# Spectral products by adding transfers, and a new order of the butterflies, in two FFT-convolution layers

## The chip, the cores and the metric

The kernel runs on one core of a Trainium2 chip. The metric is the time of one execution on the device in microseconds; runs of one kernel agree within about 0.1%, and the median of three is taken. The profile is of one execution.

## The reference

Four layers follow one another, each adding its result to `x`, which has L = 2048 rows and D = 640 columns:

- layers a and c: normalize each row, then convolve each of the 640 columns causally with its own kernel of length 2048 (a sum of 128 damped exponentials), and add a multiple of the input;
- layers b and d: normalize each row, then multi-query attention of 32 heads of width 20 (one key and value for all).

```python
Kf = rfft2(Kp[:, None, :])                # the kernel, padded to 2L
Uf = rfft2(up[:, :, None, :])             # the normalized input, padded to 2L
y = irfft2(Uf * Kf[None], s=(1, 2 * L))[:, :, 0, :L]
x = x + (y.transpose(0, 2, 1) + u * Dskip)
```

The change is in layers a and c alone. Their kernel spectra are worked out once, in layer a, and kept in DRAM.

## The kernel before

**Tiling.** The 640 columns are cut into five chunks of 128 (`NCH = 5`, `c` = 0 to 4). A chunk's spectrum is one tile `A` of 128 partitions x 16 x 256 numbers (2 MB). The 16 slots are eight sub-transforms with a real and an imaginary slot each.

**A chunk's steps**, each on its own engine:

- ScalarE scales the rows of x into a tile `xn` of which there is one buffer (`normals`, L736; 24 instructions of 128x128);
- PE multiplies `xn` by the weights `wf` (`dense`, L565; 64 matmuls, which the trace counts as 128 instructions), and ScalarE copies the four results out of PSUM into `A` (L581). Chunk 0 and the kernel's own spectra use `raw` (L538) instead, whose first butterflies (`radix`, L555) run on VectorE;
- VectorE (DVE in the profile) does the forward butterflies, `fft8(..., -1)` at L90: 16 instructions between `A`, a second tile `B` and a half-size tile `R`. Its first two read all of slots 0 to 7; its seventh is the first that writes `R`;
- VectorE multiplies by the kernel's spectrum `kh` (`product`, L750): two products into `B` and `R` and a subtraction, two products and an addition, and then the first two inverse butterflies, eight instructions of 128x2048 at L751;
- VectorE does the other inverse butterflies, `fft8(..., +1)`: 16 instructions;
- PE does the inverse matmuls with the weights `wi` (`inverse`, L764) in four groups of 16 matmuls, whose results go alternately to two PSUM banks;
- VectorE adds each group to `x` (`residual`, L782). For chunk 3 the group starts with a matmul that brings `x` in (L769), and ScalarE copies it back (L785).

**Order.** On PE, ScalarE and VectorE the instructions run in the order in which the program writes them; the other queues (SP and POOL) take theirs as they come ready. Each engine's queue is in order. `weave` (L133) puts a list of calls between the instructions of another list, at given places. `turn(g)` (L829) does the residual of group g and, for g = 0 and 1, writes PE's group g + 2. The loop at L807 does for each chunk: product and inverse butterflies (with turns 2 and 3 of the chunk before woven in), groups 0 and 1 of the inverse, forward butterflies of the next chunk (turns 0 and 1 woven in), scaling and `dense` of the chunk after next. So `dense` stands on PE behind all four inverse groups of the chunk.

**Buffers.** Two spectra `A`, two kernel spectra `kh` (loaded two chunks ahead by SP, L680), one `B`, one `R`.

**Around it.** While chunk 3 and 4 are done, ScalarE works out sums and squares of `x` for the next layer's normalization (`stats_first`, L609), and in layer a the attention weights are split into two parts on PE and ScalarE (`attn_weights`, L871; "the weight splitting"), woven into chunk 4's product. In layer a the kernel's own spectra come first (`kernel_spectra`, L685): raw transforms, butterflies and a store of each to DRAM.

Of the kernel before, what the change touches and what calls it, by code (L numbers as in the profile page):

```python
# [11 lines left out]
F32 = mybir.dt.float32  # L12
# [4 lines left out]
ALU = mybir.AluOpType  # L17
# [4 lines left out]
P = 128  # L22
# [4 lines left out]
NCH = D // DC  # L27
# [59 lines left out]
    }  # L87


def fft8(nc, A, B, R, sg):  # L90

    ADD, SUB = ALU.add, ALU.subtract
    plus, minus = (ADD, SUB) if sg < 0 else (SUB, ADD)
    calls = []

    def tt(*a):
        calls.append(lambda: nc.vector.tensor_tensor(*a))  # L100

    def stt(*a):
        calls.append(lambda: nc.vector.scalar_tensor_tensor(*a, op0=ALU.mult, op1=ADD))
# [24 lines left out]
    stt(A[:, 6:16:9], f3s, sp, f2)  # L128
    stt(A[:, 14:6:-7], f3s, sm, f2)
    return calls  # L130


def weave(calls, between):  # L133

    for i in range(len(calls) + 1):
        for n, call in between:
            if n == i or (i == len(calls) and n > i):
                call()
        if i < len(calls):
            calls[i]()  # L140


class Net:
# [394 lines left out]
    def raw(self, xn, nm):  # L538


        nc = self.nc
        Z = self.spectrum(f"z{nm}")
        for t in range(4):
            z = self.ps2(f"z{nm}_{t}")
            zv = z.rearrange("p (h c k d) -> p h c k d", h=2, c=2, k=2)
            for h in (1, 0):
                for kk in range(2):
                    for c in range(2):
                        for j in range(2):
                            nc.tensor.matmul(zv[:, h, c, kk], self.wf[:, t + 4 * h, j, c, kk],  # L550
                                             xn[:, 8 * j + t + 4 * h], start=(j == 0), stop=(j == 1))
            nc.scalar.activation(Z[:, 4 * t : 4 * t + 4].rearrange("p s d -> p (s d)"), z, AF.Copy)
        return Z

# [7 lines left out]
                    Z[:, 4 * t + 2 : 4 * t + 4], op))  # L562
        return calls

    def dense(self, xn, nm):  # L565


        nc = self.nc
        A = self.spectrum(nm)
        for t in range(4):  # L570
            z = self.ps2(f"z{nm}_{t}")
            zv = z.rearrange("p (c s k d) -> p s c k d", s=2, c=2, k=2)
            for kk in range(2):
                for c in range(2):
                    for n, (h, j) in enumerate(((1, 0), (1, 1), (0, 0), (0, 1))):
                        i = 4 * j + t
                        x = (xn[:, 8 + 2 * i : 10 + 2 * i] if h
                             else xn[:, i][:, None, :].to_broadcast([P, 2, DC]))
                        nc.tensor.matmul(zv[:, :, c, kk], self.wf[:, t + 4 * h, j, c, kk], x,  # L579
                                         start=(n == 0), stop=(n == 3))  # L580
            nc.scalar.activation(A.rearrange("p (o s) d -> p o s d", o=2)[:, :, 2 * t : 2 * t + 2],  # L581
                                 z.rearrange("p (c o e) -> p o c e", c=2, o=2), AF.Copy)
        return A
# [94 lines left out]
        nc.vector.scalar_tensor_tensor(nmr, mv[:, :, 0], -1.0, out, op0=ALU.mult, op1=ALU.mult)  # L678

    def load_spectrum(self, c):  # L680
        A = self.cvp.tile([P, 16, 256], F32, tag="kh", bufs=2, name=f"kh{c}")
        self.nc.sync.dma_start(A.rearrange("p s d -> p (s d)"), self.kh[c])
        return A

    def kernel_spectra(self):  # L685

        nc, cv = self.nc, self.cvp

        kts = cv.tile([P, 4, 16, DC], F32, tag="wi", name="kts")
        ktl = cv.tile([P, 24, DC], F32, tag="xn", name="ktl")  # L690
        ks = [kts[:, c] for c in range(4)] + [ktl[:, 0:16]]
        dsk = ktl[0:1, 16:21]
        nc.gpsimd.dma_start(dsk.rearrange("p c d -> p (c d)"), self.ins["A_Dskip"][None, :])
        for c in range(NCH):
            nc.gpsimd.dma_start(ks[c].rearrange("p t d -> p (t d)"), self.kd[c])
# [6 lines left out]
        Z = {0: self.raw(ks[0], "k0")}  # L702
        for c in range(NCH):
            if c + 1 < NCH:
                skip(c + 1)
                Z[c + 1] = self.raw(ks[c + 1], f"k{c + 1}")
            A = cv.tile([P, 16, 256], F32, tag="kh", bufs=2, name=f"kn{c}")
            weave(self.radix(Z.pop(c), A) + fft8(nc, A, self.B, self.R, -1), ())
            nc.sync.dma_start(self.kh[c], A.rearrange("p s d -> p (s d)"))

    def conv_layer(self, nm, first):
# [6 lines left out]
        with tc.manual_schedule(engines={mybir.EngineType.PE, mybir.EngineType.Activation,  # L718
# [86 lines left out]
            As[1] = self.dense(xn, f"{nm}1")  # L805
            late = []
            for c in range(NCH):  # L807
                A = As.pop(c)
                mul = product(A, khs.pop(c)) + fft8(nc, A, B, R, +1)
                if c == NCH - 1:  # L810
                    late = sorted(late + [(1 + k, a[0]) for k, a in enumerate(pieces)]
                                  + [(3 + k, a[1]) for k, a in enumerate(pieces)], key=lambda a: a[0])
                weave(mul, late)
                late = []
                if c == NCH - 2:
                    scr = new_xn("s").rearrange("p a d -> p (a d)")

                    def dump(n):
                        return scr[:, 1280 + NA * (n % 4) : 1280 + NA * (n % 4) + NA]

                    self.stats_setup(nm)
                    for g in range(3):
                        self.stats_first(g, dump)
                if c + 2 < NCH:
                    khs[c + 2] = self.load_spectrum(c + 2)
                    xn = new_xn(c + 2)
                ys = [inverse(c, g, A) for g in range(2)]

                def turn(g, c=c, A=A, ys=ys):  # L829

                    residual(c, g, ys[g])
                    if g < 2:
                        ys.append(inverse(c, g + 2, A))

                if c + 1 < NCH:
                    woven = [(5, lambda: turn(0)), (11, lambda: turn(1))]
                    if c == NCH - 2:
                        pieces = self.attn_weights(scr, nm == "a")
                        woven.append((11, lambda: self.stats_first(3, dump)))
                    weave(fft8(nc, As[c + 1], B, R, -1), woven)  # L840
                    late = [(1, lambda turn=turn: turn(2)), (2, lambda turn=turn: turn(3))]
                if c + 2 < NCH:
# [3 lines left out]
                if c + 2 == NCH - 1:  # L846
                    self.wfs.pop().close()
        turn(0)
        self.stats_base()
        self.norm_part(0, 1)  # L850
# [482 lines left out]
```

## Time and profile before

| | |
|---|---|
| median of three runs | 3069.56 us (3068.69 to 3069.82) |
| the profiled execution: its own time | 3071.17 us |
| its span, first to last instruction | 3069.4 us |
| mean granted clock of PE | 0.986 |
| layer a: first raw transform of a kernel spectrum to last inverse matmul | 344.1 to 660.1 us |
| layer c: first raw transform to last inverse matmul | 1747.5 to 1983.2 us |
| DMA traffic | 158.82 MB, mean 52 GB/s |

A line of a timeline gives the start in us from the span's start, the length, the engine, the line of the kernel, the operation, out<-in by tile names (`Aa` and `Ac` are the spectra of layers a and c), shapes and the count of instructions merged into it; in brackets stands the idle time of that engine just before, and who ended it. An fp32 matmul shows as two instructions. In a group line the last numbers are busy us, mean ns of one, and idle time before. A line of the windows view gives the window and its length, then for each engine the busy us and the count of instructions, the granted clock, the busy share of the DMA engines, and GB/s. Layers b and d are attention, where ScalarE and PE are busy throughout.

### The profile page before, as it was taken

To read this page: it belongs to the slowest core of one execution; us is meant where nothing else is said; L and a number is where in the kernel's file an instruction comes from. 1 tells how busy PE (TensorE), PEld (TensorE's weight loads), DVE (VectorE), ACT (ScalarE), POOL (GpSimd) and SP (SyncE) were. 2 spreads that over 40 slices of the span, in tenths; PEclk is the share of its full clock that TensorE was granted. 3 is DMA by queue.
4 is the path that set the end of the run, shared out by engine and by line. 5 is a ranking of instruction groups with operands and counts; after the bars stand their busy time and mean duration, and the time that the engine had idled before them with its cause. 6 is when DMAs were issued, how large, how long until landed. Compare 5 with 4: busy or idle time off the path is not lost. (4 is left out here: it accounts for less than half of the span.)

```text
span 3069.4 us, 52317 instructions
## 1 busy us (share of the span) xinstructions
PE 2874.8 (94%) x21696; PEld 1362.8 (44%) x21696; DVE 1404.4 (46%) x1793; ACT 2428.3 (79%) x2910; POOL 41.5 (1%) x113
## 2 busy tenths in 40 slices
PE   2888898989899999999999989798999999999999
PEld 0555887867323323333233479673223333333233
DVE  7888799972122232232222399922122222222223
ACT  5777343353899999999999633446999999999997
POOL 0000000000100000000000000000000000000000
PEclk9999999989999999999999999899999999999999
DMA  6010551123300010000100210132000100100100
GB/s 143 18 29 17 177 220 56 38 83 131 112 24 25 22 28 22 24 25 22 27 23 24 112 55 28 50 125 79 23 22 25 39 27 24 39 25 21 45 19 22
DMA packets 72177, 158.82 MB, mean 52 GB/s; under 512 B 21509, under 2 KB 27653, under 8 KB 67797
## 3 DMA queue, kind: packets, MB, share of 16 engines
q1 hardware_dynamic: 65880, 137.70, 14.9%
q0 software_dynamic: 4080, 16.67, 1.5%
q8 instruction: 175, 2.87, 0.4%
q10 hardware_dynamic: 1968, 0.98, 0.1%
q14 instruction: 74, 0.60, 0.1%
HBM read 95.22 MB, written 48.04 MB: 47 GB/s over the span
## 5 line engine op out<-in xcount | busy, mean ns | idle before, releaser
L1134 ACT ACTIVATE pt<-scb 128x1024 f32<-128x1024 f32 x1024 | 942.2, 1115 | 7.5 <-PE scb L1130 5.8
L1134 ACT ACTIVATE pt<-scd 128x1024 f32<-128x1024 f32 x1024 | 942.2, 1118 | 7.0 <-PE scd L1130 5.5
L1144 PE MATMUL pod<-pt,vt 128*32 128x512 f32 x4096 | 546.9, 606 | 4.4 <-DVE on L1161 0.8
L1144 PE MATMUL pob<-pt,vt 128*32 128x512 f32 x4096 | 546.9, 606 | 4.3
L1130 PE MATMUL scb<-qpb,kt 62*128 62x512 f32 x2048 | 386.0, 451 | 6.2 <-PEq L1079 5.8
L1130 PE MATMUL scd<-qpd,kt 62*128 62x512 f32 x2048 | 385.8, 451 | 5.8 <-PEq L1079 5.5
L1130 PEld LDWEIGHTS scd<-qpd,kt 62*128 62x128 f32 x2048 | 166.1, 185 | 402.0 <-ACT pt L1134 392.3
L1130 PEld LDWEIGHTS scb<-qpb,kt 62*128 62x128 f32 x2048 | 165.9, 185 | 402.1 <-ACT pt L1134 392.6
L1192 DVE TENSOR_TENSOR x<-pyd,x 128x320 f32<-128x320 f32 x146 | 71.7, 491 | 561.0 <-PE pyd L1204 561.0
L1192 DVE TENSOR_TENSOR x<-pyb,x 128x320 f32<-128x320 f32 x146 | 71.7, 491 | 547.7 <-PE pyb L1204 547.7
L1164 DVE RECIPROCAL rc<-rc 128x512 f32<-128x512 f32 x62 | 207.9, 3353 | 2.1
L1144 PEld LDWEIGHTS pob<-pt,vt 128*32 128x32 f32 x4096 | 80.7, 108 | 178.3 <-issue 160.3
L1144 PEld LDWEIGHTS pod<-pt,vt 128*32 128x32 f32 x4096 | 80.6, 108 | 177.7 <-issue 159.7
L421 PE MATMUL pk<-s,m 128*64 128x32 f32 x1280 | 130.8, 295 | 13.3 <-DVE s L412 13.3
L421 PE MATMUL pk<-c,e1r 128*64 128x32 f32 x1280 | 132.1, 297 | 11.4 <-DVE c L411 11.2
L421 PEld LDWEIGHTS pk<-c,e1r 128*64 128x64 f32 x1280 | 105.3, 221 | 79.6 <-issue 52.2
L579 PE MATMUL za<-xna,wf 128*128 128x256 f32 x512 | 113.0, 383 | 2.7 <-ACT xna L733 2.7
L421 PEld LDWEIGHTS pk<-s,m 128*64 128x64 f32 x1280 | 108.1, 226 | 15.9 <-DVE s L412 15.9
L579 PE MATMUL zc<-xnc,wf 128*128 128x256 f32 x512 | 111.5, 379 | 2.7 <-ACT xnc L733 2.7
L581 ACT ACTIVATE Aa<-za 128x1024 f32<-128x1024 f32 x16 | 16.4, 1023 | 118.3 <-PE za L579 116.9
L581 ACT ACTIVATE Ac<-zc 128x1024 f32<-128x1024 f32 x16 | 16.4, 1024 | 113.7 <-PE zc L579 113.7
L579 PEld LDWEIGHTS za<-xna,wf 128*128 128x128 f32 x512 | 98.0, 192 | 16.7 <-ACT xna L733 3.3
(308 smaller groups left out, 3272.9 us busy)
## 6 DMA issues: line engine op xcount, KB each, us to landing
kh<-kh SPq DMA_DIRECT2D x10, 2048.0 KB
kh<-kn SPq DMA_DIRECT2D x5, 2048.0 KB
qhd<-qh SPq DMA_DIRECT2D x40, 256.0 KB
qld<-ql SPq DMA_DIRECT2D x40, 256.0 KB
qpb<-qhd SPq DMA_DIRECT2D x256, 40.0 KB
qpd<-qhd SPq DMA_DIRECT2D x256, 40.0 KB
ot<-on SPq DMA_DIRECT2D x216, 40.0 KB
wf<-in_c_wf POOLq DMA_DIRECT2D x16, 512.0 KB, 7.9
```

Of the source, the lines that this page charges most:

```text
L421: nc.tensor.matmul(PK[u][64 * par : 64 * par + 64, 32 * d : 32 * d + 32], e[u][:, d, par], c[u][:, d, par], start=first, stop=not first)
L579: nc.tensor.matmul(zv[:, :, c, kk], self.wf[:, t + 4 * h, j, c, kk], x, start=(n == 0), stop=(n == 3))
L581: nc.scalar.activation(A.rearrange("p (o s) d -> p o s d", o=2)[:, :, 2 * t : 2 * t + 2], z.rearrange("p (c o e) -> p o c e", c=2, o=2), A ...
L1130: nc.tensor.matmul(sc[:, 512 * par : 512 * par + 512], kt[rows, 128 * t : 128 * t + 128], qps[nb, hg, pr][rows], start=True, stop=True)
L1134: nc.scalar.activation(pt, sc, AF.Exp, scale=SCALE)
L1144: nc.tensor.matmul(po[32 * j : 32 * j + 32], vt[:, t], pts[step, j // 2][:, 512 * (j % 2) : 512 * (j % 2) + 512], start=(t == 0), stop=(t ...
L1164: nc.vector.reciprocal(rc, rc)
L1192: nc.vector.tensor_tensor(xh, py, xh, ALU.add)
```

## The change

- **The products.** For chunks 0 to 3 `product` gives way to `spread`: four products, `R = -(A_im * kh_im)`, `kh_im = A_re * kh_im`, `A_re = A_re * kh_re`, `A_im = A_im * kh_re`, all but the first in place. The two additions are done by two transfers on the POOL queue that add into their destination: `A_re += R` after the third product, `A_im += kh_im` after the fourth. Each moves 128 x 2048 numbers (1 MB) from SBUF to SBUF; the destination is in pieces of 256 numbers. Chunk 4 keeps the old product.
- **The order.** Behind `spread` of chunk c come the forward butterflies of chunk c + 1 (with all four turns of chunk c - 1 woven in, ahead of instructions 3, 7, 11 and 15), the scaling and `dense` of chunk c + 2, and only then the rest of chunk c: `back`, which is the two first inverse butterflies into `R` and `A`, and `fft8(..., +1)` whose first two instructions read `R` in place of `A`'s lower half. Then groups 0 and 1 of chunk c's inverse. So on PE `dense(c + 2)` stands ahead of inverse(c, 0), and `dense(1)` and `dense(2)` come straight after one another. The seventh forward instruction writes `R`, which the first transfer reads; `back` reads `A`, which both write.
- **The buffers.** Three spectra (tags A0, A1, A2) and one kernel spectrum in place of two and two. The load of the next kernel spectrum waits for the second transfer, which reads `kh`. Chunk 0's raw transform and every other stored kernel spectrum use A2.
- **The end.** Turns 0 to 3 of chunk 3 are woven into chunk 4's product, at 1, 2, 4 and 5, and the weight splitting starts two places later. `stats_first` stands behind the forward butterflies of chunk 4.

```diff
-def fft8(nc, A, B, R, sg):
+def fft8(nc, A, B, R, sg, low=None):
...
-    tt(B[:, 0:4], A[:, 0:4], A[:, 4:8], ADD)
-    tt(B[:, 4:8], A[:, 0:4], A[:, 4:8], SUB)
+    low = A if low is None else low
+    tt(B[:, 0:4], low[:, 0:4], low[:, 4:8], ADD)
+    tt(B[:, 4:8], low[:, 0:4], low[:, 4:8], SUB)
...
-    def spectrum(self, nm):
-        return self.cvp.tile([P, 16, 256], F32, tag="A", bufs=2, name=f"A{nm}")
+    def spectrum(self, nm, k):
+        return self.cvp.tile([P, 16, 256], F32, tag=f"A{k}", bufs=1, name=f"A{nm}")
...
-        A = self.cvp.tile([P, 16, 256], F32, tag="kh", bufs=2, name=f"kh{c}")
+        A = self.cvp.tile([P, 16, 256], F32, tag="kh", name=f"kh{c}")
...
-            A = cv.tile([P, 16, 256], F32, tag="kh", bufs=2, name=f"kn{c}")
+            A = cv.tile([P, 16, 256], F32, tag=("kh", "A2")[c % 2], name=f"kn{c}")
...
-            Z = self.raw(xn, f"{nm}0")
-            As = {0: self.spectrum(f"{nm}0")}
-            khs = {c: self.load_spectrum(c) for c in range(2)}
+            Z = self.raw(xn, f"{nm}0", 2)
+            As = {0: self.spectrum(f"{nm}0", 0)}
+            khs = {0: self.load_spectrum(0)}
...
+            def spread(A, kh):
...
+                ops = [lambda: nc.vector.scalar_tensor_tensor(R, m(A, 1), -1.0, m(kh, 1),
+                                                              op0=ALU.mult, op1=ALU.mult),
+                       lambda: tt(m(kh, 1), m(A, 0), m(kh, 1), ALU.mult),
+                       lambda: tt(m(A, 0), m(A, 0), m(kh, 0), ALU.mult),
+                       lambda: nc.gpsimd.dma_start(m(A, 0), R, accum_op=ALU.add),
+                       lambda: tt(m(A, 1), m(A, 1), m(kh, 0), ALU.mult),
+                       lambda: nc.gpsimd.dma_start(m(A, 1), m(kh, 1), accum_op=ALU.add)]
+                for op in ops:
+                    op()
+
+            def back(A):
+                return [lambda: tt(R, A[:, 0:8], A[:, 8:16], ALU.add),
+                        lambda: tt(A[:, 8:16], A[:, 0:8], A[:, 8:16], ALU.subtract)] + fft8(
+                            nc, A, B, R, +1, low=R)
+
+            turn = None
             for c in range(NCH):
                 A = As.pop(c)
-                mul = product(A, khs.pop(c)) + fft8(nc, A, B, R, +1)
                 if c == NCH - 1:
-                    late = sorted(late + [(1 + k, a[0]) for k, a in enumerate(pieces)]
-                                  + [(3 + k, a[1]) for k, a in enumerate(pieces)], key=lambda a: a[0])
-                weave(mul, late)
...
+                    late = [(1, lambda turn=turn: turn(0)), (2, lambda turn=turn: turn(1)),
+                            (4, lambda turn=turn: turn(2)), (5, lambda turn=turn: turn(3))]
+                    late = sorted(late + [(3 + k, a[0]) for k, a in enumerate(pieces)]
+                                  + [(5 + k, a[1]) for k, a in enumerate(pieces)], key=lambda a: a[0])
+                    weave(product(A, khs.pop(c)) + fft8(nc, A, B, R, +1), late)
+                else:
+                    spread(A, khs.pop(c))
+                    khs[c + 1] = self.load_spectrum(c + 1)
+                    woven = [] if turn is None else [
+                        (n, lambda turn=turn, g=g: turn(g)) for g, n in enumerate((2, 6, 10, 14))]
+                    weave(fft8(nc, As[c + 1], B, R, -1), woven)
+                    if c + 2 < NCH:
+                        xn = new_xn(c + 2)
+                        for t in range(4):
+                            normals(c + 2, t)
+                        As[c + 2] = self.dense(xn, f"{nm}{c + 2}", (c + 2) % 3)
...
+                        for g in range(4):
+                            self.stats_first(g, dump)
+                        pieces = self.attn_weights(scr, nm == "a")
+                    weave(back(A), ())
                 ys = [inverse(c, g, A) for g in range(2)]
...
-                if c + 1 < NCH:
-                    woven = [(5, lambda: turn(0)), (11, lambda: turn(1))]
...
-                    weave(fft8(nc, As[c + 1], B, R, -1), woven)
-                    late = [(1, lambda turn=turn: turn(2)), (2, lambda turn=turn: turn(3))]
-                if c + 2 < NCH:
-                    for t in range(4):
-                        normals(c + 2, t)
-                    As[c + 2] = self.dense(xn, f"{nm}{c + 2}")
```

More of the change, by code (lines that the diff above doesn't have):

```diff
@@ L533, in load_weights, with raw @@
                           self.ins[name][:, t * 1024 : (t + 1) * 1024])
-    def spectrum(self, nm):
-        return self.cvp.tile([P, 16, 256], F32, tag="A", bufs=2, name=f"A{nm}")
-    def raw(self, xn, nm):
+    def spectrum(self, nm, k):
+        return self.cvp.tile([P, 16, 256], F32, tag=f"A{k}", bufs=1, name=f"A{nm}")
+    def raw(self, xn, nm, k):
         nc = self.nc
-        Z = self.spectrum(f"z{nm}")
+        Z = self.spectrum(f"z{nm}", k)
         for t in range(4):
@@ L563, in radix, with dense @@
         return calls
-    def dense(self, xn, nm):
+    def dense(self, xn, nm, k):
         nc = self.nc
-        A = self.spectrum(nm)
+        A = self.spectrum(nm, k)
         for t in range(4):
@@ L701, in kernel_spectra @@
         skip(0)
-        Z = {0: self.raw(ks[0], "k0")}
+        Z = {0: self.raw(ks[0], "k0", 0)}
         for c in range(NCH):
@@ L705, in kernel_spectra @@
                 skip(c + 1)
-                Z[c + 1] = self.raw(ks[c + 1], f"k{c + 1}")
-            A = cv.tile([P, 16, 256], F32, tag="kh", bufs=2, name=f"kn{c}")
+                Z[c + 1] = self.raw(ks[c + 1], f"k{c + 1}", (c + 1) % 2)
+            A = cv.tile([P, 16, 256], F32, tag=("kh", "A2")[c % 2], name=f"kn{c}")
             weave(self.radix(Z.pop(c), A) + fft8(nc, A, self.B, self.R, -1), ())
@@ L804, in conv_layer @@
             weave(self.radix(Z, As[0]) + fft8(nc, As[0], B, R, -1), ())
-            As[1] = self.dense(xn, f"{nm}1")
-            late = []
+            As[1] = self.dense(xn, f"{nm}1", 1)
+            def spread(A, kh):
[8 more added lines that the diff above has]
+                    op()
@@ new lines, in conv_layer, with dump @@
+                    late = sorted(late + [(3 + k, a[0]) for k, a in enumerate(pieces)]
[12 more added lines that the diff above has]
+                        As[c + 2] = self.dense(xn, f"{nm}{c + 2}", (c + 2) % 3)
+                    if c + 2 == NCH - 1:
+                        self.wfs.pop().close()
+                    if c == NCH - 2:
+                        scr = new_xn("s").rearrange("p a d -> p (a d)")
+                        def dump(n):
+                            return scr[:, 1280 + NA * (n % 4) : 1280 + NA * (n % 4) + NA]
+                        self.stats_setup(nm)
+                        for g in range(4):
+                            self.stats_first(g, dump)
+                        pieces = self.attn_weights(scr, nm == "a")
+                    weave(back(A), ())
```

16 lines of the change are left out of this document (removed).

## The prediction

> **What bounds the kernel now.** The page gives the shares first.
>
> ```profile
> PE 2874.8 (94%) x21696; PEld 1362.8 (44%) x21696; DVE 1404.4 (46%) x1793; ACT 2428.3 (79%) x2910; POOL 41.5 (1%) x113
> ```
>
> These are averages over stages of different kinds; the change touches only the two convolution layers, about 344 to 660 us (layer a) and 1747 to 1983 us (layer c). So I cut those into stretches of one chunk (busy time by engine; the columns are PE, PEld, DVE, ACT, POOL, then the granted clock, DMA share and GB/s).
>
> ```profile
> 495.01:537.16 42.15, 42.15 (x259) 38.69 (x258) 41.94 (x45) 13.33 (x28) 0.00 (x0) 1.00 0.14 51
> 537.16:579.31 42.15, 42.15 (x259) 38.69 (x258) 41.94 (x45) 13.33 (x28) 0.00 (x0) 1.00 0.14 51
> 1819.40:1861.55 42.15, 42.15 (x259) 38.69 (x258) 41.94 (x45) 13.33 (x28) 0.00 (x0) 1.00 0.14 50
> ```
>
> A middle chunk takes 42.15 us, and **both** PE and DVE are busy for all of it. Each is therefore a bound by itself. Next the order of events on DVE and on PE in layer a (start, length, engine, line, tiles, count, and the idle time before where there was any).
>
> ```profile
> 453.38 2.29 DVE L751 TENSOR_TENSOR B<-Aa,kh 128x2048 f32<-128x2048 f32 x1
> 466.95 4.49 DVE L751 TENSOR_TENSOR Aa<-B 128x2048 f32<-128x2048 f32 x2
> 471.48 3.56 DVE L100 TENSOR_TENSOR B<-Aa 128x1024 f32<-128x1024 f32 x4
> 482.31 3.56 DVE L100 TENSOR_TENSOR B<-Aa 128x1024 f32<-128x1024 f32 x4
> 494.44 2.29 DVE L751 TENSOR_TENSOR B<-Aa,kh 128x2048 f32<-128x2048 f32 x1
> 619.67 2.29 DVE L751 TENSOR_TENSOR B<-Aa,kh 128x2048 f32<-128x2048 f32 x1
> ```
>
> ```profile
> 438.88 28.96 PE L579 MATMUL za<-xna,wf 128*128 128x256 f32 x126 [0.46 <-ACT xna L733]
> 475.70 9.21 PE L776 MATMUL ya<-Aa,wi 128*128 128x128 f32 x64 [7.85 <-DVE Aa L100]
> 495.01 27.79 PE L579 MATMUL za<-xna,wf 128*128 128x256 f32 x128
> 522.64 14.68 PE L776 MATMUL ya<-Aa,wi 128*128 128x128 f32 x128
> 537.15 27.79 PE L579 MATMUL za<-xna,wf 128*128 128x256 f32 x128
> 623.26 2.07 PE L769 MATMUL ya<-x,ident 128*128 128x512 f32 x2 [7.32 <-ACT x L785]
> 633.69 0.60 PE L908 MATMUL pw<-kv,ident 128*128 128x260 f32 x2
> 645.60 14.46 PE L776 MATMUL ya<-Aa,wi 128*128 128x128 f32 x128
> ```
>
> On DVE the eight product instructions take 471.48 - 453.38 = 18.1 us (2.26 each), the inverse butterflies 482.31 - 471.48 = 10.83. From the first product of chunk 0 (453.38) to that of chunk 4 (619.67) are 166.3 us without a gap. On PE a dense forward transform takes 522.64 - 495.01 = 27.6 us and a chunk's inverse matmuls 537.15 - 522.64 = 14.5: together the same 42.15. PE has gaps only at the ends: 7.85 us before the first inverse, 7.32 before the pair at 623.26.
>
> **The change, in a middle chunk.** DVE loses two of the eight 2048-element instructions, the two additions. Left are four products, 9.05 (the one with a scalar is the same kind as the rest: the butterflies' scalar form has the same mean as their plain one), the forward butterflies 10.83, four residuals 2.4 (0.60 from start to start) and then two instructions plus the inverse butterflies, 4.5 + 10.83 = 15.35.
>
> ```profile
> L103 DVE SCALAR_TENSOR_TENSOR Aa<-B 128x512 f32<-128x512 f32 x40 | 25.0, 686 | 0.3
> L787 DVE TENSOR_TENSOR x<-ya,x 128x512 f32<-128x512 f32 x16 | 10.9, 683 | 2.7 <-PE ya L776 2.7
> ```
>
> The sum is 37.6 us in place of 42.15: 4.5 less, eight times in the kernel, 36 us of DVE work. But PE's 27.6 + 14.5 does not change, and its queue is in order. So **the middle stays at 42.15 us a chunk**, and what the change is worth is decided at the ends of each layer.
>
> **The chain in layer a.** Up to 453.38 nothing moves on the path: the only spectrum now loaded ahead waits for a store from its buffer, and lands by about 451.
>
> ```profile
> 437.73 0.33 SPq L709 DMA_DIRECT2D kh<-kn  x1
> 444.05 0.32 SPq L682 DMA_DIRECT2D kh<-kh  x1
> ```
>
> The 2 MB store issued at 437.73 was over by 444.05, 6.3 us, and the same again for the load gives 450.4. Chunk 0's raw transform now goes to the third buffer, free when an earlier store ends (429.34, when the load that waited for it went out before); that is 3 us after ScalarE's first copy, and DVE takes no raw result until 437.62:
>
> ```profile
> 429.34 0.33 SPq L682 DMA_DIRECT2D kh<-kh  x1
> ```
>
> ```profile
> 426.37 1.01 ACT L552 ACTIVATE Aza<-za 128x1024 f32<-128x1024 f32 x1
> 437.62 4.89 DVE L560 TENSOR_TENSOR Aa<-Aza 128x512 f32<-128x512 f32 x8
> ```
>
> The products of chunk 0 end at 462.4. Now the forward butterflies of chunk 1 come next, and they need dense(1), which had been hidden behind chunk 0's product and inverse butterflies.
>
> ```profile
> 467.89 1.02 ACT L581 ACTIVATE Aa<-za 128x1024 f32<-128x1024 f32 x1 [5.88 <-PE za L579]
> 468.81 0.87 ACT L733 ACTIVATE xna<-x,nmra,rsa 128x128 f32<-128x128 f32 x2
> ```
>
> Its last eviction ends at 468.9, so DVE waits 6.5 us, which is new. Forward(1) ends at 479.8, back(0) at 495.2, the products of chunk 1 at 504.2. PE goes straight to dense(2) when the first six scalings of 0.386 us are done, 471.1, and ends it at T2 = 498.9; inverse(0) groups 0 and 1 end at 506.2. The first residual sits behind two forward instructions, 504.2 + 2.2 + 0.6 = 507.0; groups 2 and 3 follow to 514.3, dense(3) ends at T3 = 541.9. From there PE has no wait: at T + 7.3 groups 0 and 1 are done, and DVE's first two residuals come at about T + 4.5 and T + 8.1, ahead of need. T4 = 541.9 + 42.15 = 584.1. Forward(4) is held by the residual of PE's last group at T4 + 14.5, then 0.6 + 1.2: 600.4. Back(3) ends at 615.8, so the product of chunk 4, unchanged, starts at **615.8 instead of 619.67**.
>
> For the tail I take layer c, where DVE alone sets it.
>
> ```profile
> 1777.76 2.29 DVE L751 TENSOR_TENSOR B<-Ac,kh 128x2048 f32<-128x2048 f32 x1
> 1944.09 2.29 DVE L751 TENSOR_TENSOR B<-Ac,kh 128x2048 f32<-128x2048 f32 x1
> ```
>
> ```profile
> 1767.93 27.46 PE L579 MATMUL zc<-xnc,wf 128*128 128x256 f32 x126 [0.45 <-ACT xnc L733]
> 1966.51 16.73 PE L776 MATMUL yc<-Ac,wi 128*128 128x128 f32 x128 [8.38 <-DVE Ac L100]
> ```
>
> From the last product's start to the last inverse matmul are 1983.24 - 1944.09 = 39.15 us. In layer a that gives 655.0 against 645.60 + 14.46 = 660.06: **5.1 us less**. PE's own way there is shorter: inverse(3) from about 609, 4 x 4.5, then the weight splitting from 633.7 to 645.6 (11.9) and 14.5 come to 653.5. The statistics on ScalarE, which made the 7.32 us gap, now lie behind back(3).
>
> **Layer c** starts from dense(1)'s end, 1795.39, 17.6 us after the first product instead of 14.5. The same chain (600.4 - 467.84 = 132.6, then 15.35) puts the last product at 1943.3 against 1944.09: **0.8 us less**. Together 5.9.
>
> **PE's clock.** PE now idles 3.3 us before dense(2). The gaps of 2.3 us before dense(1) went two ways (columns: PE, clock, DMA):
>
> ```profile
> 439.70:441.70 2.00, 2.00 (x6) 0.50 1.07 451
> 1768.70:1770.70 2.00, 2.00 (x11) 1.00 0.03 8
> ```
>
> Layer a paid 28.96 - 27.46 = 1.5 us for the clock of 0.50, layer c nothing. I charge half of it per layer: 1.5 in all. Net **4.4 us less**.
>
> **The price of the adding transfers.** No transfer in this trace adds. The nearest rows are plain 1 MB loads on the same queue (median us to landing), and their issue.
>
> ```profile
> kts<-kd POOLq DMA_DIRECT2D x4, 1024.0 KB, 9.3
> ktl<-kd POOLq DMA_DIRECT2D x1, 1024.0 KB, 5.1
> ```
>
> ```profile
> 338.63 2.11 POOL L695 DMA_DIRECT2D kts<-kd  x4
> ```
>
> Alone 5.1; as 2 MB took 6.3, about 3.0 of it is moving and 2.1 is overhead. Below, adding costs no more than copying: the first lands X = 5.1 us after its issue, the second, behind it on the same queue, Y = 8.1 after that same moment. Above, I take four times the moving (two reads and a write one after another, and pieces of 1 KB, not 8): 12 us each, X = 14.1, Y = 26.1. I take two reads per byte, 6.0 each, nearest to the row that moves 2 MB: X = 8.1, Y = 14.1. Four in a row (median 9.3) fit 2.1 + 3.0 for each one ahead. POOL's issue is 2.11 / 4 = 0.53 us, and behind its waits for the products stands nothing but a memset for the weight splitting, due after 626; SP's load of the next spectrum waits for the second transfer, needs some 7 us, and is due 15.35 us after back starts.
>
> The Trainium skill, page "Collectives: The Full Stack", section on the bandwidth ceiling, says that a reduce in the DMA engines is slower than a copy by its second source read, not by the add. By it the moving would be 6.0 and the sum the same; no run here shows it yet.
>
> What the path allows: R is needed again at forward instruction 7, A at back. Round one chunk, X + 29.6 (ten forward instructions, two residuals, back, three products) and Y + 22.2 must stay under 42.15, so X < 12.5, Y < 20. In chunk 1, where DVE is late, the first transfer goes out at 501.9 and back(1) is ready at 517.4; a Y over 15.5 is paid from DVE's slack until the products of chunk 2 (541.8) pass T3 + 1.2, and later waits add up. I find no loss up to **Y = 18**, and some 6.5 us in all for each us above (three to four chunks, two layers).
>
> **The rivals.**
> 1. *Slow adding, slower kernel.* Place: DVE before back and before forward instruction 7. It eats the 4.4 us at Y = 18.7 and passes +0.2% (6.1 us) at Y = 19.6. With 10.5 us of moving each (Y = 23.1) it costs 6.5 x 5.1 = 33: 3098. For it: 1 KB pieces, and a read that must precede the write. Against: the two-read estimate leaves 4 us. Chance 0.27.
> 2. *DVE holds the transfers up.* If POOL cannot write its descriptors while DVE runs, both transfers start only when DVE stops at forward instruction 7. A chunk is then 37.6 + 8.1 = 45.7: forward(4) at 468.9 + 3 x 45.7 - 2.4 = 603.6, the last product 36.7 later at 640.3 (20.6 late), in layer c 23.5 late: 3112. Against: nothing in the trace shows DVE holding POOL. Chance 0.07. The Trainium skill, page "SBUF — State Buffer", the "DVE blocks DMA" trap, states such a lock for two-port copies, and for tensor_tensor only against GpSimd's reads; no run here shows it.
> 3. *DVE alone is the bound* and all 36 us come off: 3034. For: DVE is as full as PE. Against: PE's rows without a gap. Chance 0.05.
>
> **How the numbers follow.** The profiled execution ran 3071.17 us around a span of 3069.4, the median of the runs is 3069.56. 3071.17 - 4.4 = 3066.8 profiled, **3065.2** against the median. My own errors at the ends (clock, latencies) leave 3062 to 3067.5 for this case; chance 0.61, of it 0.14 beyond -0.2%. About 0.2% is what a measurement here can tell from no change. Faster: 0.14 + 0.05 = 0.19. Same: 0.47 + 0.04 from rival 1 = 0.51. Slower: 0.23 + 0.07 = 0.30. The range 3061 to 3105 leaves out rival 3, rival 2 and rival 1's worst part, about 0.2.
>
> **What would show it.** Right: PE without gaps from dense(3) to inverse(2), DVE idle about 2 us a chunk before the forward butterflies with dense's eviction as releaser, the last products near 616 and 1943, no wait for a DMA of A or R. Rival 1 shows as DVE waiting for a transfer into A before back; rival 2 as transfers that move nothing until DVE stops; rival 3 as chunks of 38 us. The forecast is wrong if a chunk in the middle isn't 42 us.

## The result, and the profile after

The changed kernel takes 3067.91 us (median of 20 runs, 3064.54 to 3070.28); beside it the kernel before took 3070.02 (20 runs, 3068.51 to 3073.63). The ratio is 0.9992, 95% interval 0.9985 to 0.9999: within 0.2% of no change, and on the faster side of it by some 2 us where 4.4 were forecast. The profiled execution ran 3068.54 us around a span of 3066.8.

The page of the changed kernel, its totals (busy time and share by engine) and, below, its software DMA queue (packets, MB, share of 16 engines' span):

```profile
span 3066.8 us, 52364 instructions
PE 2871.7 (94%) x21696; PEld 1360.6 (44%) x21696; DVE 1370.1 (45%) x1777; ACT 2429.1 (79%) x2910; POOL 66.7 (2%) x129
q0 software_dynamic: 20720, 33.45, 5.3%
```

VectorE is busy 34.3 us less than before (1404.4), close to the 36 us of additions. The span is 2.6 us shorter. So the work went, and the time did not go with it. The stretches of one middle chunk, two in layer a and two in layer c, say why (busy time by engine PE, PEld, DVE, ACT, POOL, then granted clock, DMA share, GB/s):

```profile
512.99:554.91 41.92, 41.92 (x258) 38.61 (x257) 39.84 (x47) 13.33 (x28) 3.08 (x2) 1.00 0.56 110
554.91:596.83 41.92, 41.92 (x258) 38.61 (x257) 37.27 (x42) 13.68 (x39) 3.43 (x3) 1.00 0.58 120
1836.45:1878.37 41.92, 41.92 (x259) 38.61 (x258) 39.46 (x46) 13.33 (x28) 3.09 (x2) 1.00 0.55 109
1878.37:1920.30 41.93, 41.93 (x258) 38.58 (x256) 34.91 (x39) 13.67 (x38) 3.11 (x2) 1.00 0.53 132
```

TensorE is busy for all of each stretch. VectorE now has room there, and TensorE leaves it none to use: a chunk takes 41.92 us, where it took 42.15. So the ends of the layers decide. VectorE in both layers, the first product of chunk 0, the waits, and the first product of chunk 4 (L752):

```profile
452.40 2.29 DVE L810 SCALAR_TENSOR_TENSOR R<-Aa,kh 128x2048 f32<-128x2048 f32 x1
467.41 3.56 DVE L100 TENSOR_TENSOR B<-Aa 128x1024 f32<-128x1024 f32 x4 [5.87 <-ACT Aa L582]
510.56 1.29 DVE L100 TENSOR_TENSOR R<-Aa 128x512 f32<-128x512 f32 x2 [1.95 <-DMA Aa<-R]
592.78 1.29 DVE L100 TENSOR_TENSOR R<-Aa 128x512 f32<-128x512 f32 x2 [2.18 <-DMA Aa<-R]
615.60 2.29 DVE L752 TENSOR_TENSOR B<-Aa,kh 128x2048 f32<-128x2048 f32 x1
...
1772.22 2.29 DVE L810 SCALAR_TENSOR_TENSOR R<-Ac,kh 128x2048 f32<-128x2048 f32 x1
1790.95 3.56 DVE L100 TENSOR_TENSOR B<-Ac 128x1024 f32<-128x1024 f32 x4 [9.58 <-ACT Ac L582]
1834.12 1.29 DVE L100 TENSOR_TENSOR R<-Ac 128x512 f32<-128x512 f32 x2 [1.97 <-DMA Ac<-R]
1919.04 1.30 DVE L100 TENSOR_TENSOR R<-Ac 128x512 f32<-128x512 f32 x2 [5.01 <-DMA Ac<-R]
1941.86 2.29 DVE L752 TENSOR_TENSOR B<-Ac,kh 128x2048 f32<-128x2048 f32 x1
```

And TensorE at the two ends:

```profile
640.11 14.46 PE L777 MATMUL ya<-Aa,wi 128*128 128x128 f32 x128
1935.14 5.35 PE L777 MATMUL yc<-Ac,wi 128*128 128x128 f32 x32 [11.81 <-DVE Ac L100]
1964.29 16.80 PE L777 MATMUL yc<-Ac,wi 128*128 128x128 f32 x128 [10.51 <-DVE Ac L100]
```

Two executions don't start a layer at the same microsecond, so a layer is measured from its own first product: to the first product of chunk 4, and to the last inverse matmul's end.

| | a: to last product | a: to the end | c: to last product | c: to the end |
|---|---|---|---|---|
| before | 166.29 | 206.68 | 166.33 | 205.48 |
| forecast | 162.4 | 201.6 | 165.5 | 204.7 |
| after | 163.20 | 202.17 | 169.64 | 208.87 |

Layer a gained 4.5 us, near the forecast 5.1. Layer c **lost 3.4** where 0.8 were to be gained. The row that differs is the wait of 5.01 us at 1919.04: VectorE stands before the forward instruction that overwrites `R`, until the adding transfer that reads `R` has landed. The queues show what that transfer met. POOL in the changed kernel, its issues of the last pair in layer c, and SP's loads near them:

```profile
1904.37 1.55 POOL L814 DMA_DIRECT2D Ac<-R  x1 [36.58 <-DVE Ac L813]
1906.50 1.56 POOL L816 DMA_DIRECT2D Ac<-kh  x1 [0.57 <-DVE Ac L815]
```

```profile
1906.19 0.33 SPq L901 DMA_DIRECT2D wh<-whd  x1
```

and SP in the kernel before:

```profile
1931.52 0.32 SPq L883 DMA_DIRECT2D wh<-whd  x1
```

The load of the attention weights (128 x 3460 numbers, 1.8 MB) is released by the end of the last dense transform. The new order ends that transform earlier, at 1906, while the back half of chunk 3 still lies ahead. So the load now goes out between the two adding transfers. That this is the cause is only a reading so far; the runs below test it.

### The profile page after: what moved, and what is told of

It reads as the page before. It is cut to its first block, busy times and chain, and to the rows that moved or that the text cites. A ratio compares the mean times of both kernels' runs of the same rounds, so it can differ in the third digit from the quotient of the medians.

```text
span 3066.8 us, 52364 instructions
## 1 busy us (share of the span) xinstructions
PE 2871.7 (94%) x21696; PEld 1360.6 (44%) x21696; DVE 1370.1 (45%) x1777; ACT 2429.1 (79%) x2910; POOL 66.7 (2%) x129
## 3 DMA queue, kind: packets, MB, share of 16 engines
q0 software_dynamic: 20720, 33.45, 5.3%
## 5 line engine op out<-in xcount | busy, mean ns | idle before, releaser
L580 PEld LDWEIGHTS zc<-xnc,wf 128*128 128x128 f32 x512 | 96.8, 190 | 19.7 <-ACT xnc L734 6.8
L1222 PE MATMUL pyb<-wo,ot 128*32 128x320 f32 x1168 | 105.3, 432 | 0.0
```

The lines of the kernel that those rows point to most:

```text
L1222: nc.tensor.matmul(py[j : j + m], o[:, 128 * i + j : 128 * i + j + m], w[:, 320 * half : 320 * half + 320], start=start, stop=stop)
```

## The experiments

Theory: in the middle TensorE is the bound and hides all that VectorE and the transfers do; what the change is worth is set at the ends of the layers, where layer c pays for a collision with the weight load. Rivals: the transfers themselves eat the 36 us; the order alone makes the gain; the long wait has another cause. Ratios are to the kernel before, with 95% intervals.

**1. No adding transfers.** The two additions are left out of chunks 0 to 3.

```diff
-                       lambda: nc.gpsimd.dma_start(m(A, 0), R, accum_op=ALU.add),
                        lambda: tt(m(A, 1), m(A, 1), m(kh, 0), ALU.mult),
-                       lambda: nc.gpsimd.dma_start(m(A, 1), m(kh, 1), accum_op=ALU.add)]
```

> The changed kernel without its two adding transfers: the two additions of the complex products of chunks 0 to 3 are left out, in both layers. Theory (TensorE is the bound of the middle chunks, the transfers are hidden there): the middle chunks stay at 41.9 us; only the waits for a transfer before the inverse butterflies go, of which those of chunk 3 count, about 1 us in layer a (the last group of inverse products starts earlier by no more than the butterflies do) and about 4 us in layer c; in all about 5 us less than the changed kernel, 3063 us. Rival (the transfers take the 36 us that VectorE saved, by contention on the memory or by their waits): 15 to 30 us less than the changed kernel.

Measured: 3065.77 us (3062.15 to 3067.69), ratio 0.9982 (0.9973 to 0.9991). The layers: a 200.27 to the end, c 165.54 to the last product and 205.06 to the end, so 1.9 and 3.8 us less than the changed kernel. The 5.7 us do not all show in the time: from the end of layer c to the end of the span are 1089.0 us here and 1085.7 in the changed kernel, a part that no edit touches. That spread of about 3 us between executions is why the tables here go by layers. A middle chunk, from one dense transform to the next on TensorE, still takes 41.92 us:

```profile
513.89 27.79 PE L580 MATMUL za<-xna,wf 128*128 128x256 f32 x128
...
555.81 27.79 PE L580 MATMUL za<-xna,wf 128*128 128x256 f32 x128
```

The 15 to 30 us of the rival are not there: **taking the transfers away altogether frees only the waits at the ends.**

**2. The additions on VectorE again, in the new order.**

```diff
-                       lambda: nc.gpsimd.dma_start(m(A, 0), R, accum_op=ALU.add),
+                       lambda: tt(m(A, 0), m(A, 0), R, ALU.add),
                        lambda: tt(m(A, 1), m(A, 1), m(kh, 0), ALU.mult),
-                       lambda: nc.gpsimd.dma_start(m(A, 1), m(kh, 1), accum_op=ALU.add)]
+                       lambda: tt(m(A, 1), m(A, 1), m(kh, 1), ALU.add)]
```

> The changed kernel with the two additions on VectorE, in place, where the two adding transfers were issued; order and buffers as changed. Theory (the order sets the middle chunks, the additions count only at the end of a layer, where VectorE ends last): the middle chunks stay at 41.9 to 43 us, VectorE busy through them; the last product of each layer about 5 us later than in the changed kernel less the transfer's wait that goes: 5 to 10 us more than the changed kernel, 3073 to 3078 us. Rival (the order and the third buffer alone make the gain, the transfers do nothing): equal to the changed kernel, 3068 us.

Measured: 3077.77 us, ratio 1.0025 (1.0016 to 1.0034). A middle chunk of this kernel:

```profile
548.73:590.65 41.92, 41.92 (x258) 38.66 (x257) 41.68 (x45) 13.32 (x28) 0.00 (x0) 1.00 0.14 51
```

On TensorE the chunk is the same 41.92 us with VectorE at 41.68 as with VectorE at 35 to 40. VectorE itself is a little slower than that: 42.27 us from its first product of chunk 2 (538.46) to that of chunk 3 (580.73). The last products come at 169.84 and 173.36, 6.6 and 3.7 us later than in the changed kernel. Part of it is a wait that the full VectorE queue hands to TensorE in front of chunk 0's third inverse group, since that group's PSUM bank is freed by a residual on VectorE:

```profile
511.51 9.76 PE L777 MATMUL ya<-Aa,wi 128*128 128x128 f32 x64 [5.97 <-DVE x L788]
```

So **the order alone is a loss** of 8 us; the adding transfers bring it back, at the ends.

**3. Half of the dense stage's matmuls left out, in both kernels.** TensorE then is no bound in the middle, and what VectorE saves must show.

```diff
-                    for n, (h, j) in enumerate(((1, 0), (1, 1), (0, 0), (0, 1))):
+                    for n, (h, j) in enumerate(((1, 0), (0, 0))):
```

> The kernel before with half of the dense stage's matmuls left out (the products of the second of the two row blocks), so that TensorE has some 28 us a middle chunk instead of 42. Theory (VectorE needs some 42 us a chunk in the kernel before, so both engines are near the bound there): the middle chunk stays near 42 us and the time falls by no more than a few us, 3066 to 3069 us. Rival (VectorE has room): the chunks shorten to 35 us or less and the time falls by 40 us or more.

> The changed kernel with the same half of the dense stage's matmuls left out. Theory (the change took 4.5 us a chunk from VectorE, and TensorE's 42 us hid it): now the saving shows, the middle chunk falls to 38 to 40 us, set by VectorE with its waits for the transfers, and the kernel is some 20 us shorter than the kernel before with the same part left out, 3045 to 3050 us. Rival (the transfers, or their contention with VectorE, cost what the additions cost): no shorter than the kernel before with the same part left out, 3066 us.

Measured: 3066.45 us (ratio 0.9990, 0.9981 to 0.9999) and 3053.61 us (0.9946, 0.9931 to 0.9961). One middle chunk of the kernel before with half, then of the changed kernel with half:

```profile
516.91:559.06 42.15, 31.35 (x193) 28.97 (x193) 41.94 (x45) 13.33 (x29) 0.00 (x0) 0.86 0.14 50
```

```profile
515.62:554.28 38.66, 30.03 (x194) 28.19 (x193) 36.55 (x42) 13.32 (x28) 3.08 (x2) 0.91 0.52 105
```

The kernel before does not notice that half of the dense matmuls are gone and TensorE is busy for 31.35 us in place of 42.15: VectorE alone holds it at 42.15. The changed kernel does: 38.66. Both bounds of the old middle are thus real, and lifting one of them shows nothing until the other is lifted too. The two differ by 12.8 us, not by the 20 that I expected. From the first product to the last are 166.31 us in the one and 158.47 in the other (layer a), 7.8 less and not four times 4.5, because the waits for the transfer now lie on the path:

```profile
471.41 1.29 DVE L100 TENSOR_TENSOR R<-Aa 128x512 f32<-128x512 f32 x2 [3.27 <-DMA Aa<-R]
478.26 2.29 DVE L821 TENSOR_TENSOR R<-Aa 128x2048 f32<-128x2048 f32 x1 [0.62 <-DMA Aa<-kh]
510.61 1.29 DVE L100 TENSOR_TENSOR R<-Aa 128x512 f32<-128x512 f32 x2 [1.98 <-DMA Aa<-R]
550.28 1.29 DVE L100 TENSOR_TENSOR R<-Aa 128x512 f32<-128x512 f32 x2 [1.97 <-DMA Aa<-R]
589.98 1.29 DVE L100 TENSOR_TENSOR R<-Aa 128x512 f32<-128x512 f32 x2 [1.99 <-DMA Aa<-R]
```

3.27 + 0.62 + 1.98 + 1.97 + 1.99 = 9.8 of the 18 us. That leaves 8.2, against 7.8 measured. Layer c is much the same: 166.33 us in the one and 158.46 in the other.

**4. The adding transfers in the old order.**

```diff
+                mul = (product(A, kh) + fft8(nc, A, B, R, +1) if c == NCH - 1
+                       else spread(A, kh) + back(A))
...
-                    spread(A, khs.pop(c))
```

> The order and the two buffers of the kernel before, with the adding transfers: the inverse butterflies of a chunk follow its product at once, so that they wait for the second transfer. Theory (a transfer pair takes 16 us from the first issue, and only the next chunk's forward butterflies hide it): about 14 us of wait a chunk, the middle chunk near 52 us, TensorE idle for 10 of them, 3140 to 3155 us. Rival (the transfers cost nothing where they stand): 4.5 us a chunk less on VectorE, 3034 to 3070 us.

The two buffers for spectra and two for kernel spectra are those of before as well. Measured: 3143.44 us, ratio 1.024 (1.021 to 1.027). A middle chunk on TensorE (the one before it took 52.35 us), and VectorE's wait in two of them:

```profile
557.36:608.03 50.67, 44.35 (x259) 40.31 (x257) 36.61 (x43) 13.34 (x28) 3.08 (x2) 0.97 0.41 83
```

```profile
528.45 2.29 DVE L819 TENSOR_TENSOR R<-Aa 128x2048 f32<-128x2048 f32 x1 [13.91 <-DMA Aa<-kh]
579.97 2.29 DVE L819 TENSOR_TENSOR R<-Aa 128x2048 f32<-128x2048 f32 x1 [13.92 <-DMA Aa<-kh]
```

The transfers are slow: VectorE waits 14 us for them behind the last product, and the new order is what hides them. Neither half of the change stands alone: the order without the transfers costs 8 us, the transfers without the order 74.

**5. Layer c's weight loads later.** ScalarE writes one element of each target behind chunk 4's first products, and the loads wait for it.

```diff
+                        late = sorted(late + [(2, lambda: self.attn_weights(scr, False))],
+                                      key=lambda a: a[0])
...
+            for w, n in ((wh, 0), (wl, 0)):
+                nc.scalar.activation(w[0:1, 0, 0:1], self.ident[0:1, 0:1], AF.Copy)
```

> The changed kernel, where in layer c the two big attention weight loads are released only behind the product of chunk 4 (ScalarE writes one element of each target first), so that they no longer share the DMA engines with the adding transfers of chunk 3. Theory: the wait for the transfer before the inverse butterflies of chunk 3 in layer c falls from 5.0 to about 2 us and the layer ends 3 us earlier: 3065 us. Rival (the long wait has another cause, such as the descriptor writing): the wait stays at 5 us, 3068 us.

Measured: 3062.78 us, ratio 0.9978 (0.9969 to 0.9987). VectorE at the same place, with nothing before the instruction that writes `R`:

```profile
1906.54 2.36 DVE L100 TENSOR_TENSOR B<-Ac 128x1024 f32<-128x1024 f32 x2 [1.20 <-ACT Ac L582]
...
1913.23 1.28 DVE L100 TENSOR_TENSOR R<-Ac 128x512 f32<-128x512 f32 x2
...
1937.05 2.29 DVE L752 TENSOR_TENSOR B<-Ac,kh 128x2048 f32<-128x2048 f32 x1
```

The wait is gone, not only shortened to 2 us as I had expected, and layer c's last product comes 1937.05 - 1771.51 = 165.54 us after its first, which is the forecast to a tenth. **The collision was layer c's whole loss.** The first transfer of the pair, issued at 1903.67 here, had landed by 1913.23, so in 9.6 us at most; beside the load it took from 1904.37 to 1919.04, 14.7.

**6. Layer a as changed, layer c as before.**

```diff
-        net.conv_layer("c", False)
+        net.conv_layer_old("c", False)
```

> Layer a as in the changed kernel, layer c with the order, the products and the two buffers of the kernel before. Theory (layer a gains some 5 us and layer c gives some 3 us back): 3064.5 us, 3 us less than the changed kernel. Rival (the gain and the loss lie elsewhere, or layer c's loss comes from a later start that moves with it): 3068 us, as the changed kernel.

Measured: 3064.20 us, ratio 0.9982 (0.9973 to 0.9991). As expected: layer a carries the gain (202.40 us to its end), and layer c is back at 205.57, as in the kernel before. With the load out of the way (run 5) the new order is at least as good in layer c as the old.

**7. Late loads in layer a too.**

```diff
-        nc.gpsimd.memset(kv, 0.0)
+        nc.scalar.activation(kv.rearrange("p k n -> p (k n)"), scr[:, 1280:1540], AF.Copy, scale=0.0)
+        for o in (0, D):
+            nc.scalar.activation(scr[0:1, o : o + 1], self.ident[0:1, 0:1], AF.Copy)
```

> The changed kernel with the late weight loads in both layers: in layer c as in the run before (behind the product of chunk 4), in layer a the loads of kv and of the first two pieces of wq are released by small ScalarE writes behind its sums for the normalization, some 25 us later than now and 20 us before TensorE reads them. Theory (a transfer with nothing beside it lands within the forward butterflies, the waits of the last chunk come from loads that share the DMA engines): the 2.3 us wait before chunk 3's inverse butterflies in layer a goes to under 0.5 us, as it went in layer c, and the layer ends 2 us earlier: 3061 us. Rival (layer a's wait is the adding transfer's own time, or the late loads make TensorE wait for the pieces): 3063 us or more.

Measured: 3063.34 us, ratio 0.9980 (0.9971 to 0.9989). In layer a the wait has gone. Chunk 3's first transfer, which took 12.3 us from issue to landing in the changed kernel and in run 5, takes 9.5:

```profile
591.82 1.28 DVE L100 TENSOR_TENSOR R<-Aa 128x512 f32<-128x512 f32 x2
```

The layer ends 200.60 us after its first product, 2.5 less than in run 5 (203.06) and 1.6 less than in the changed kernel, and the last product stands at 615.63 - 453.28 = 162.35, where 162.4 were forecast. By the mechanism the theory holds; by the time the rival's number came, since the medians of runs 5 and 7 do not show 2 us (their ranges are 3061.51 to 3068.15 and 3060.93 to 3066.00).

**8. Chunk 2's residual off VectorE as well.** A candidate that builds on the finding: only what stands on VectorE behind the last dense transform counts. Beside the lines below, ScalarE's sums are laced between its four copies.

```diff
-                whole = c == NCH - 2
+                whole = NCH - 3 <= c <= NCH - 2
...
-                if c == NCH - 2:
+                if NCH - 3 <= c <= NCH - 2:
                     nc.scalar.activation(stream(c, g), y, AF.Copy)
```

> The run with the late loads in both layers, and chunk 2's residual is added by TensorE (identity products into the same PSUM group) and copied by ScalarE, as chunk 3's already is, its four groups laced with ScalarE's sums. Theory (VectorE's chain behind the last dense group sets the end of each layer, TensorE idles 11 us there): four additions of 0.6 us go from that chain; two of them stand ahead of the transfer's wait and only lengthen it, so 1.2 to 2.4 us a layer: 3057 to 3059 us. Rival (ScalarE or the transfer is next late): as the run before, 3061 us.

Measured: 3056.68 us (3055.00 to 3058.18), ratio 0.9957 (0.9944 to 0.9971): faster than both kernels. Layer a ends at 198.62, layer c at 202.17, 2.0 and 2.8 us less than in run 7. Expected were 1.2 to 2.4 a layer, so layer c gained a little more. VectorE's short waits for TensorE ahead of each residual went too (0.15 to 0.48 us each, 1.46 in run 7's layer c), which the expectation had not counted. The two layers make 4.8 of the 6.7 us between the medians of runs 7 and 8; the rest lies outside the layers, where executions vary. VectorE now waits for the transfer again, so that is next late:

```profile
1907.95 1.29 DVE L100 TENSOR_TENSOR R<-Ac 128x512 f32<-128x512 f32 x2 [1.86 <-DMA Ac<-R]
```

| to the last product / to the end | layer a | layer c |
|---|---|---|
| changed kernel | 163.20 / 202.17 | 169.64 / 208.87 |
| 1, no transfers | 162.06 / 200.27 | 165.54 / 205.06 |
| 2, added on VectorE | 169.84 / 209.13 | 173.36 / 212.29 |
| 5, late load in c | 163.81 / 203.06 | 165.54 / 204.89 |
| 6, layer c as before | 163.29 / 202.40 | 166.35 / 205.57 |
| 7, late loads in both | 162.35 / 200.60 | 165.53 / 204.97 |
| 8, and residual moved | 159.40 / 198.62 | 163.27 / 202.17 |

## Why the prediction was right, and where its terms were off

**The middle stays TensorE's: right.** Chunks of 41.92 us without a gap, with 35 to 40 us of VectorE in them and with 41.7 (run 2), show that the 36 us could not be collected in the middle. In run 3, where TensorE has room, 12.8 us of them appear; in layer a the waits for the transfers take 9.8 of the other 23. Rival 3 (3034 us) falls with that.

One reading needs a correction. The prediction took each of the two engines as a bound of 42.15 us. Run 3 shows that VectorE alone holds the old chunk there, and in the new order TensorE needs 41.92. In the kernel before, TensorE's weight loads wait for one of VectorE's residuals inside the inverse matmuls:

```profile
533.48 3.65 PEld L776 LDWEIGHTS ya<-Aa,wi 128*128 128x128 f32 x32 [0.15 <-DVE x L787]
```

So the old middle was VectorE's by 0.23 us a chunk, and only that much could be collected there. That such waits make up all of the 0.23 us is likely but not shown.

**The chain in layer a: right.** The new wait for dense(1) measured 5.87 us (6.5 forecast), the last product 163.20 after the first (162.4). The 0.8 between them goes with the wait of 2.18 us before `R`, and run 7 shows the cause: the loads of `kv` and of the first pieces of `wq`, which go out as soon as the last dense transform has ended. Without them beside the transfer the chain comes out at 162.35. The tail, taken as 39.15 us from layer c of the kernel before, was 38.97 in layer a and 39.23 in layer c.

**Layer c: the step that failed.** "The same chain puts the last product at 1943.3 against 1944.09: 0.8 us less" took over layer a's chain with transfers that have the DMA engines to themselves. But behind the last dense transform of layer c goes a load of 1.8 MB, and the prediction listed what was queued behind POOL's issues and behind SP's load of the next spectrum, not what SP would issue earlier because the transform ends earlier. It cost 3.8 to 4.1 us (runs 1 and 5). The row was in the trace of before: `wh` at 1931.52, on the heels of the last dense transform.

The Trainium skill has the rule that was missing, page "DMA: Bandwidth & Descriptors", section "Issuing engines are not separate DMA queues": transfers started by different engines run on the same 16 DMA engines and interleave. The trace agrees: 9.6 us alone, 14.7 beside a load that another engine issued.

**"No wait for a DMA of A or R": wrong, at no cost in the middle.** X, the time from the first transfer's issue to its landing, was forecast at 8.1 us, and Y, from the same moment to the second's landing, at 14.1. The DMA groups of the changed kernel's trace that add (KB each, median us from issue to landing):

```profile
Aa<-R POOLq DMA_DIRECT2D x4, 1024.0 KB, 9.8
Aa<-kh POOLq DMA_DIRECT2D x4, 1024.0 KB, 14.3
Ac<-R POOLq DMA_DIRECT2D x4, 1024.0 KB, 9.5
Ac<-kh POOLq DMA_DIRECT2D x4, 1024.0 KB, 14.3
```

These medians mix transfers that had company with transfers that had none. Without company the first lands in 9.5 to 10.1 us. Run 4 shows an undisturbed pair: issued at 512.87 and 514.84, landed 9.5 and 13.5 us after their own issues, so X = 9.5 and Y = 15.5. The difference, 6.0 us, is the moving of one MB: the estimate of two reads per byte was right. The miss is the overhead, 3.5 us in place of 2.1, of which POOL's issue, 1.55 us and not 0.53, makes up 1.0. With X = 9.5 VectorE waits some 2 us in chunks 1 to 3. That idle time was forecast, but before the forward butterflies and with dense's eviction as its releaser; it shows so only in chunk 3 (1.70 us in layer a, 1.21 in layer c), while in the middle it stands before `R` with the transfer as its releaser. The bounds of the prediction (X under 12.5, no loss up to Y = 18) held: run 1 gained nothing in the middle. Run 4's wait of 13.9 us is about Y less the last product, which still ran for 1.7 us after the first issue. Rival 1 needed a Y of 18.7. That a reduce is slower than a copy by its second source read, as the page "Collectives: The Full Stack" of the Trainium skill has it in the section on the bandwidth ceiling, agrees with 6.0 us a MB against some 3.1 for plain loads; the runs don't separate the read from the add.

**VectorE does not hold the transfers up: rival 2 falls.** Chunk 1 of layer a in the changed kernel, POOL's issue and VectorE's last instruction ahead of the wait for it:

```profile
501.06 1.54 POOL L814 DMA_DIRECT2D Aa<-R  x1 [37.66 <-issue]
```

```profile
507.92 0.68 DVE L788 TENSOR_TENSOR x<-ya,x 128x512 f32<-128x512 f32 x1
```

VectorE ran on to 508.6, and the transfer had landed by 510.56, 9.5 us after its issue and 2 us after VectorE stopped, as fast as any. The lock that the Trainium skill's page "SBUF — State Buffer" describes in its "DVE blocks DMA" trap is stated for copies with two ports, and none of it shows beside these tensor_tensor instructions.

**The clock.** The 1.5 us that I charged for a low clock in dense(2) do not show in the layers. TensorE of the changed kernel at dense(2) and inverse(0), in layer a and in layer c:

```profile
468.58 0.70 PE L580 MATMUL za<-xna,wf 128*128 128x256 f32 x2 [2.26 <-ACT xna L734]
469.73 29.15 PE L580 MATMUL za<-xna,wf 128*128 128x256 f32 x126 [0.46 <-ACT xna L734]
498.72 14.46 PE L777 MATMUL ya<-Aa,wi 128*128 128x128 f32 x128
...
1792.12 0.70 PE L580 MATMUL zc<-xnc,wf 128*128 128x256 f32 x2 [2.26 <-ACT xnc L734]
1793.28 27.46 PE L580 MATMUL zc<-xnc,wf 128*128 128x256 f32 x126 [0.46 <-ACT xnc L734]
1829.20 7.41 PE L777 MATMUL yc<-Ac,wi 128*128 128x128 f32 x64 [1.32 <-DVE x L788]
```

Layer a lost 1.7 us to the lower clock behind the gap (granted clock 0.52 from 470.5 to 472.5 us); layer c did not (1.00 from 1792 to 1794), and waited 1.32 us for a residual instead. From dense(2)'s first matmul to the end of inverse(0) are 44.6 us in the one and 44.5 in the other.

**In sum:** -4.5 us in layer a for -5.1, +3.4 in layer c for -0.8, and none of the 1.5 us of clock. The span shows -2.6 and not the sum, -1.1: in this pair of executions 1.0 us more was saved ahead of layer a's first product and 0.4 behind layer c. Such parts vary: over all runs the time between the two layers lies between 1114.9 and 1117.7 us. The measured 3067.91 us lies just past the 3062 to 3067.5 that the prediction gave its own case. It stays inside the wider range because that range had room for slow transfers; that it also covers a collision that nobody foresaw is luck.

## What to carry to other kernels

Where two engines are both full for the length of a stage, taking work from one gives next to nothing there (0.23 us a chunk here, for 4.5 taken away); look at the ends of the stage, where one of them is alone, and move work off that engine there (run 8: 2.4 us a layer of residual additions moved from the end gained 2.0 and 2.8 us; the 18 us a layer of product additions had gained 4.5 in one layer).

A transfer that hides behind a stretch of work hides only if nothing else is released into that stretch: whatever ends earlier by the change releases its waiters earlier, and loads of megabytes are among them. List, for each instruction that the change moves forward, every DMA that waits for it.

## What the runs showed of the hardware

- An adding transfer from SBUF to SBUF of 1 MB in pieces of 1 KB lands 9.5 to 10.1 us after its issue with no load beside it, and the second of a pair 15.5 us after the first one's issue (run 4; 15.4 to 16.9 in the changed kernel), so each moves for some 6.0 us. By estimate a plain 1 MB load on the same queue moves for 3.1: four queued ones in the kernel before, issued from 338.6 to 340.2, landed between 344.1 and 353.3. Beside a 1.8 MB load the adding transfer took 14.7 us (layer c), beside the smaller loads in layer a 12.3.
- Issuing one takes POOL 1.55 us (0.53 for a plain 1 MB load), and the queue's packets rose from 4080 to 20720 for 16 of them, 1040 a transfer.
- In the kernels with the new order and all their matmuls, with the transfers (41.92 us) or without them (runs 1 and 2, 41.92), the middle chunk is 0.23 us shorter on TensorE than in the old order (42.15), all of it in the inverse matmuls (14.45 against 14.68 us a chunk), where the old order has TensorE wait for a residual.
